# Four of 32 float64 weight tiles loaded and decoded inside the first block of the second MLP

## The chip, the cores and the metric

The kernel runs on one core of one Trainium2 chip. The metric is device time in microseconds (us) of one execution, taken as the median of several runs. Every time below that is not a median of runs comes from one profiled execution of the kernel before.

## The reference

The computation has three parts on 1536 tokens (2 batches of 768) with 512 features. Retention attention gives the tokens. A mixture of 8 experts (first matrix 512x1024, second 1024x512) takes them, each token going to one expert. A second MLP, which all tokens pass, ends it:

```python
def _moe2_ref(x, w_in, w_out):          # x 1536x512, w_in 512x2048, w_out 2048x512
    h = x @ w_in
    g = h - np.tanh(h)
    return (g @ w_out).astype(np.float32)
```

`w_in` and `w_out` come as float64, since they are scaled by a numpy double. The chip's engines work in float32, so the kernel builds a float32 value from the two 32-bit words of each double.

## The kernel before

**Weight tiles.** `w_in` is cut into 16 tiles of 128 columns and `w_out` into 16 tiles of 128 rows. Tile 2f belongs to `w_in`, tile 2f+1 to `w_out`. Each is 128 partitions by 512 values, 512 KB as float64. Decoding one takes a load into one of two `raw` buffers (`decode_load`), two ScalarE operations for the sign (Identity L132, Sign L133) and two VectorE integer operations for the bits (L135, L136) in `decode_math`, and then in `decode_end` a ScalarE Abs (L144) and a GpSimd multiply (L145) that gives the tile `dw`.

**Splits.** Matmuls of the second MLP run in three passes on a high and a low part of each operand. ScalarE casts a decoded tile to its high part `mh` and VectorE subtracts that to give `ml`: in the expert stage in `m_split` (by L153), in the MLP in `high` and `low` (L1025, L1032).

**Stages.** Attention and routing run first, then a loop of 64 expert steps n (8 experts by 8 slices of the hidden width), then the second MLP. The order of instructions on each engine is the order in which they are written (manual schedule). Decoding is spread over attention (5 tiles) and the expert loop: every fourth step below 16, then every second one. The last four tiles, 28 to 31, are fetched in steps 52 to 58 and decoded in steps 55 to 61. Steps 48 to 63 also split tiles 0 to 15.

**The second MLP.** It has three blocks of 512 tokens (w = 0, 1, 2), each with 16 units f of the hidden width, 48 units n in all. For unit n, F(n) (`m_first`, 12 matmuls of 512 columns at L923) makes the hidden values `mhp` from tile 2f. A chain of five ScalarE operations (`g_head`, `g_body`: Square L932, Square L934, Square L942, Tanh L944, Relu L948) and five VectorE operations (L954, L958, L960, L961, L964) makes g. ScalarE casts g to `gh` (L976) and VectorE makes `gl` (L983), both issued inside the chain of unit n+1. S(n) (`m_second`, 12 matmuls at L1003) uses `gh`, `gl` and tile 2f+1. TensorE's order is F0, F1, F2, F3, S0, S1, F4, S2, F5, S3, F6, S4 and so on.

The place of `gl` in the VectorE order depends on the unit. For chains 1 to 4 (the argument `early`) it stands after the first of the five operations; from chain 5 on it stands after the fourth. A list `fill` holds small VectorE jobs. The first two in it are done after the first and the second operation of the next chain, the rest at its end:

```python
        dve.scalar_tensor_tensor(out=s1, in0=s1, scalar=B1, in1=u, ...)   # L954
        gap()                                  # one job of fill
        if last and early:
            g_low(*last)                       # gl of the unit before
        dve.scalar_tensor_tensor(out=s2, in0=s2, scalar=B2, in1=s1, ...)  # L958
        gap()                                  # one job of fill
```

In the kernel before, the jobs are the `low` splits of tiles 16 to 31. Two tiles per unit are split after chains 5 to 12 (`high` on ScalarE right after the chain, `low` in the next chain), by the rule that 2n+8 tiles are split by unit n. All tiles share a pool of 74 slots of 2 KB per partition.

Of the kernel before, what the change touches and what calls it, by code (L numbers as in the profile page):

```python
# [7 lines left out]
F32 = mybir.dt.float32  # L8
F32R = mybir.dt.float32r
I32 = mybir.dt.int32  # L10
U32 = mybir.dt.uint32
BF16 = mybir.dt.bfloat16
ACTF = mybir.ActivationFunctionType
ALU = mybir.AluOpType
# [9 lines left out]
SGN = 768.0  # L24
# [3 lines left out]
def retention_moe_mlp(ctx: ExitStack, tc: tile.TileContext, q, k, v, lam, w_gate, w1, w2, w_in, w_out, out):  # L28
    nc = tc.nc
    pe, act, dve, pool, sp = nc.tensor, nc.scalar, nc.vector, nc.gpsimd, nc.sync  # L30
    B, H, S, D = q.shape
    NT, DM = out.shape
    E, _, F = w1.shape
# [4 lines left out]
    KD = DM // 128  # L38
    NTT = NT // 128
    EF = F // 128  # L40
    NF = FF // 128
    CAP = 256

    WIDE = (240, 240, 220, 212, 206, 200, 196, 192)
    WT = WIDE[0]
# [9 lines left out]
    def slot(shape, dtype, name):  # L55
        return slp.tile(shape, dtype, tag="sl", name=name)

    def bank(shape, name):
        return ps.tile(shape, F32, tag="ps", name=name)
# [38 lines left out]
    idx = const.tile([128, NTT], I32, name="idx")  # L98
    ysort = const.tile([128, KD, NT + CAP], F32, name="ysort")

# [14 lines left out]
    dec = {}  # L115

    def decode_load(i):
        r = raws[i % 2]
        if i % 2 == 0:
            f = i // 2  # L120
            src = w_in.bitcast(I32)[:, f * 256:(f + 1) * 256].rearrange("(k p) (f t) -> p k f t", p=128, t=2)
            sp.dma_start(out=r, in_=src)
        else:
            f = i // 2
            src = w_out.bitcast(I32)[f * 128:(f + 1) * 128, :].rearrange("p (k f t) -> p k f t", k=KD, t=2)
            sp.dma_start(out=r, in_=src)
# [21 lines left out]
    def split(src, name, new=slot, shape=(128, 512)):  # L148
        shape = list(shape)
        hi = new(shape, F32R, name + "h")  # L150
        lo = new(shape, F32R, name + "l")
        act.copy(out=hi, in_=src)  # L152
        dve.tensor_tensor(out=lo, in0=src, in1=hi.bitcast(F32), op=ALU.subtract)  # L153
        return hi, lo
# [312 lines left out]
    def setup_late():  # L467
# [12 lines left out]
        for e in range(E):  # L480
            pool.memset(wide_f[:, e:e + 1], float(WIDE[e]))
        pool.iota(slots_i, pattern=[[1, CAP]], base=1, channel_multiplier=0)
        dve.tensor_copy(out=slots, in_=slots_i)
# [8 lines left out]
    ebase_i = const.tile([128, E], I32, name="ebase_i")  # L492
    slots_both = slot([128, 2, CAP], F32, "slots")
    slots, slots_i = slots_both[:, 0, :], slots_both[:, 1, :].bitcast(I32)
# [24 lines left out]
    def check_counts():  # L519
        cm = sm([128, E], F32, "cm")  # L520
        dve.tensor_tensor(out=cm, in0=byrank[:, 0, :], in1=wide_f, op=ALU.is_gt)
        cx = sm([128, 1], F32, "cx")
        dve.tensor_reduce(out=cx, in_=cm, axis=AX.X, op=ALU.max)
        few = sm([128, 1], F32, "few")
        dve.tensor_reduce(out=few, in_=ct, axis=AX.X, op=ALU.min)
        dve.scalar_tensor_tensor(out=over, in0=few, scalar=128.0, in1=cx, op0=ALU.is_lt, op1=ALU.max)
# [87 lines left out]
    def first_key(t):  # L614
        key = sm([128, 1], F32, "key")
        dve.scalar_tensor_tensor(out=key, in0=lgs[t][:, 1, 0:1], scalar=1.0, in1=ohs[:, t, 0:1], op0=ALU.add, op1=ALU.mult)
        perm = slot([128, CAP], F32, "perm")
        dve.tensor_scalar(out=perm, in0=slots, scalar1=key, scalar2=None, op0=ALU.is_equal)
# [21 lines left out]
    def e_first(*ns, wd=None):  # L640
# [20 lines left out]
        for n, hs, ls, hp in tiles:  # L661
            if n % 2 == 1:
                for g in range(2):
                    ews.pop((n // 2, g))
            hb = slot([128, 2, CAP], F32R, "hb")
            hh, hl = hb[:, 0, 0:wd], hb[:, 1, 0:wd]
# [6 lines left out]
    def e_second(n, col=None, wd=None):  # L673
# [4 lines left out]
        if f == 0:  # L678
            ys[e] = [bank([128, 2, CAP], "yp") for _ in range(KD)]
        for kk in range(KD):  # L680
# [24 lines left out]
    def y_split(w):  # L705
        r = []
        o, width = wins[w]
        per = 512 // width
        for kk in range(0, KD, per):
            hi, lo = split(ysort[:, kk:kk + per, o:o + width], "y", shape=[128, per, width])  # L710
            r += [(hi[:, i, :], lo[:, i, :]) for i in range(per)]
        yhl[w] = r
# [4 lines left out]
    nd = [0]  # L717

    nl = [0]

    def decode_fetch():
        if nl[0] < min(nd[0] + 2, 2 * NF):
            decode_load(nl[0])
            nl[0] += 1

    def decode_step():
        if nd[0] < 2 * NF:
            decode_math(nd[0])
            nd[0] += 1

# [4 lines left out]
    with tc.manual_schedule():  # L735
# [53 lines left out]
        t = NTT - 1  # L789
# [46 lines left out]
    pre = [0]  # L836
# [14 lines left out]
    with tc.manual_schedule():  # L851
        LAG = 2
        for n in range(NE + LAG):
            if n < NE:
                if n == 40:
                    check_counts()
                if n == 4:
                    token_table()
                if n >= 6 and n % 2 == 0 and n < 6 + 2 * (NTT + 1):
                    token_scatter((n - 6) // 2)  # L860
                if n == 1 or n % EF == 0 and 0 < n // EF < E - 1:
                    x_load(n // EF + 1)
                fetch(n)
                if n == 0:
                    e_split1(1, 0)
                    e_first(0, 1)
                elif n > 1:
                    e_first(n)
                if n % 2 == 0:
                    e_split1(n // 2 + 1, 1)  # L870
                else:
                    e_split1((n + 3) // 2, 0)
                e_split2(n)
                if n % EF == 4 and n // EF + 1 < E:
                    x_trans(n // EF + 1, rows_of(n // EF + 1))
                decode_flush()
                if n % (4 if n < 16 else 2) == 1:
                    decode_step()
                if n % (4 if n < 16 else 2) == 0:
                    decode_fetch()  # L880
                if n >= NE - 16 and pre[0] < nd[0] - 3:
                    m_split(pre[0])
                    pre[0] += 1
            if n == 0:
                finish_routing()
            if n >= LAG and (n < 4 or (n - LAG) % EF > 0):
                if n > 4 and (n - LAG) % EF == 1:
                    e_second(n - LAG - 1)
                e_second(n - LAG)
        while nd[0] < 2 * NF:  # L890
            decode_fetch()
            decode_step()
            decode_flush()
# [120 lines left out]
    def second_mlp(fresh):  # L1014
        seq = []
        for w, (o, width) in enumerate(wins):
            per = 512 // width
            units = [tuple(range(f, f + per)) for f in range(0, NF, per)]
            seq += [(w, fs) for fs in units]
        LAG = 2  # L1020

        def high(i):
            w = dec[i]
            hi = slot([128, 512], F32R, "mh")
            act.copy(out=hi, in_=w.rearrange("p k f -> p (k f)"))  # L1025
            whl[i] = hi

        def low(i):
            w = dec.pop(i)
            hi = whl[i]  # L1030
            lo = slot([128, 512], F32R, "ml")
            dve.tensor_tensor(out=lo, in0=w.rearrange("p k f -> p (k f)"), in1=hi.bitcast(F32), op=ALU.subtract)  # L1032
            whl[i] = (hi, lo)

        y_split(0)
        while fresh and pre[0] < 2:
            m_split(pre[0])
            pre[0] += 1
        steps = []
        for n in range(len(seq)):  # L1040
            steps.append(("F", n))
            if n >= LAG:
                steps.append(("S", n - LAG))
        n = len(seq)
        steps += [("S", i) for i in range(n - LAG, n)]
        i = steps.index(("F", n - 1))
        assert steps[i - 1] == ("S", n - 4)
        steps[i - 1:i + 1] = [("F", n - 1), ("S", n - 4), ("G", n - 1)]
        a, b = steps.index(("S", 0)), steps.index(("F", LAG + 1))
        steps[a], steps[b] = steps[b], steps[a]  # L1050
        fill = []
        for kind, n in steps:
            if kind == "S":
                m_second(*seq[n], fresh)
                continue
            w, fs = seq[n]
            if kind == "F":
                m_first(w, fs)
                if n + 1 < len(seq) and seq[n + 1][0] != w:
                    y_split(w + 1)  # L1060
                if n == len(seq) - 1:
                    continue
            g_head(w, fs)
            g_body(w, fs, fill, seq[n - 1] if n else None, n <= 4)
            if fresh:
                while pre[0] < min(2 * n + 8, 2 * NF):
                    high(pre[0])
                    fill.append(lambda i=pre[0]: low(i))
                    pre[0] += 1
            if n == len(seq) - 1:  # L1070
                g_high(w, fs)
                g_low(w, fs)
# [130 lines left out]
```

## Time and profile before

| | us |
|---|---|
| median of 3 runs | 554.06 |
| lowest and highest run | 551.78, 557.68 |
| profiled execution, its own time | 554.32 |
| its span (first to last instruction) | 552.6 |
| TensorE busy in the span | 527.9 (96%) |
| VectorE busy | 422.2 (76%) |
| ScalarE busy | 356.7 (65%) |
| GpSimd busy | 114.6 (21%) |

The profile is one execution seen by the hardware profiler. TensorE's busy time has modelled ends, so a busy TensorE is not one at its peak; what can be read surely is when it sat idle and who ended that. The expert loop ends and the second MLP starts near 273 us of the span; the first block of the MLP (units 0 to 15) lasts until about 356 us.

### The profile page before, as it was taken

What the parts mean: (1) busy time and instruction counts of PE and PEld (TensorE: products, weight loads), DVE (VectorE), ACT (ScalarE), POOL (GpSimd) and SP (SyncE); (2) the same over time, 40 slices, a digit from 0 to 9 for tenths busy, and PEclk for the clock granted to TensorE, in tenths of its full rate; (3) what the DMA queues carried; (4) which work ended last, traced back from release to release, by engine and by line L of the source; (5) the groups of instructions that cost most, each with busy time, mean ns of one, the idle gap of its engine ahead of it and who ended that gap; (6) DMA issues with size and microseconds to landing.
All of it is one profiled execution on the core that took longest, in us unless ns stands there. A gap on an engine that the chain in (4) does not pass through costs nothing.

```text
span 552.6 us, 9795 instructions
## 1 busy us (share of the span) xinstructions
PE 527.9 (96%) x3373; PEld 457.7 (83%) x3373; DVE 422.2 (76%) x814; ACT 356.7 (65%) x734; POOL 114.6 (21%) x163
## 2 busy tenths in 40 slices
PE   6999998899999899999899999999999999999991
PEld 6888777899999899999788888888888888888881
DVE  5877976889786657799978889887767687767670
ACT  2456755677686667789776787856565667565650
POOL 2256852324253222222200000002000003000002
PEclk7899998999999999999999999999999999999996
DMA  5999868599999999997000000001000001000002
GB/s 146 235 275 259 240 206 282 173 278 216 279 346 268 311 315 315 297 299 252 1 2 1 1 0 1 1 17 61 1 1 2 0 1 76 1 1 0 2 0 81
DMA packets 75411, 72.41 MB, mean 131 GB/s; under 512 B 30127, under 2 KB 60847, under 8 KB 75353
## 3 DMA queue, kind: packets, MB, share of 16 engines
q1 hardware_dynamic: 73001, 65.40, 41.0%
q0 software_dynamic: 2352, 6.31, 3.2%
q8 instruction: 28, 0.46, 0.4%
q14 instruction: 30, 0.25, 0.1%
HBM read 63.29 MB, written 8.39 MB: 130 GB/s over the span
## 4 chain that ended last, share of the span: by engine, by line
PE 66%; issue 16%; DMA 6%; DVE 5%; ACT 3%; POOL 2%; SPq 1%; DVEq 0%; ACTq 0%; POOLq 0%
PE mhp L923 17%; PE outp L1003 16%; PE yp L684 7%; PE ehp L651 7%; PE yp L683 4%; DMA raw<-in_moe_w_out_dram 3%; PE op L348 2%; PE ehp L658 2%; PE sp L300 2%; PE ehp L660 2%; PE ehp L659 2%; DMA k<-in_k_dram 1%; PE op L337 1%; POOL out_dram L68 1%; PE xtp L577 1%
## 5 line engine op out<-in xcount | busy, mean ns | idle before, releaser
L684 PE MATMUL yp<-hb,w2h 128*128 128x480 f32 (+6 forms) x256 | 83.8, 376 | 0.0
L932 ACT ACTIVATE u<-mhp 128x512 f32<-128x512 f32 x48 | 28.7, 597 | 83.0 <-PE mhp L923 82.9
L683 PE MATMUL yp<-hb,w2l 128*128 128x240 f32 (+6 forms) x256 | 73.2, 286 | 4.7 <-DVE w2l L153 2.4
L923 PE MATMUL mhp<-yh,mh 128*128 128x512 f32 x192 | 75.5, 393 | 0.9 <-ACT yh L152 0.8
L1003 PE MATMUL outp<-mh,gh 128*128 128x512 f32 x192 | 75.1, 396 | 0.0
L923 PE MATMUL mhp<-yh,ml 128*128 128x512 f32 x192 | 75.0, 390 | 0.0
L1003 PE MATMUL outp<-mh,gl 128*128 128x512 f32 x192 | 74.9, 395 | 0.0
L1003 PE MATMUL outp<-ml,gh 128*128 128x512 f32 x192 | 74.9, 395 | 0.0
L954 DVE SCALAR_TENSOR_TENSOR s<-s,u 128x512 f32<-128x512 f32 x48 | 33.2, 691 | 47.1 <-ACT s L934 47.1
L145 POOL TENSOR_TENSOR dw<-da,sg 128x512 f32<-128x512 f32 x32 | 43.2, 1349 | 113.7 <-ACT da L144 90.3
L68 POOL DMA_INDIRECT out_dram<-ysort,idx x12 | 11.7, 974 | 262.0 <-ACT ysort L1008 258.3
L651 PE MATMUL ehp<-xh,w1r 128*128 128x212 f32 (+4 forms) x320 | 60.2, 333 | 0.0
L153 DVE TENSOR_TENSOR w2l<-w2r,w2h 128x512 fp32r<-128x512 f32 x64 | 54.5, 852 | 3.2
L651 PEld LDWEIGHTS ehp<-xh,w1r 128*128 128x128 f32 x320 | 55.8, 190 | 0.1
L683 PEld LDWEIGHTS yp<-hb,w2l 128*128 128x128 f32 x256 | 49.7, 194 | 6.0 <-DVE w2l L153 3.2
L923 PE MATMUL mhp<-yl,mh 128*128 128x512 f32 x192 | 51.4, 390 | 0.0
L684 PEld LDWEIGHTS yp<-hb,w2h 128*128 128x128 f32 x256 | 49.2, 192 | 1.9
L923 PEld LDWEIGHTS mhp<-yh,mh 128*128 128x128 f32 x192 | 36.1, 188 | 10.5 <-ACT yh L152 2.5
L1003 PEld LDWEIGHTS outp<-mh,gl 128*128 128x128 f32 x192 | 36.2, 189 | 9.5 <-DVE gl L983 0.3
L1003 PEld LDWEIGHTS outp<-ml,gh 128*128 128x128 f32 x192 | 36.1, 188 | 8.6
L923 PEld LDWEIGHTS mhp<-yh,ml 128*128 128x128 f32 x192 | 36.0, 188 | 7.7
L1003 PEld LDWEIGHTS outp<-mh,gh 128*128 128x128 f32 x192 | 36.0, 188 | 7.7
(158 smaller groups left out, 1160.2 us busy)
## 6 DMA issues: line engine op xcount, KB each, us to landing
w1r<-in_moe_w_dram SPq DMA_DIRECT2D x64, 256.0 KB, 6.1
w2r<-in_moe_w_dram SPq DMA_DIRECT2D x64, 256.0 KB, 6.7
raw<-in_moe_w_in_dram SPq DMA_DIRECT2D x16, 512.0 KB, 4.3
raw<-in_moe_w_out_dram SPq DMA_DIRECT2D x16, 512.0 KB, 7.2
q<-in_q_dram SPq DMA_DIRECT2D x12, 256.0 KB, 7.2
v<-in_v_dram SPq DMA_DIRECT2D x12, 256.0 KB, 5.4
k<-in_k_dram SPq DMA_DIRECT2D x11, 256.0 KB, 5.6
xr<-xs_d SPq DMA_DIRECT2D x8, 256.0 KB, 5.3
```

The costliest lines, as they stand in the source:

```text
L68: ins = pool.indirect_dma_start(out=dst[:, :], out_offset=bass.IndirectOffsetOnAxis(ap=ix.bitcast(U32), axis=0), in_=src, in_offset=None)
L145: pool.tensor_tensor(out=w, in0=a.bitcast(F32), in1=sg, op=ALU.mult)
L153: dve.tensor_tensor(out=lo, in0=src, in1=hi.bitcast(F32), op=ALU.subtract)
L300: pe.matmul(sps[j][:, hp, :], lhsT=kt[js, hp, :], rhs=qt[hp // 2][js, hp % 2, :], start=True, stop=True)
L348: pe.matmul(op[64 * j:64 * j + 64, hp, :], lhsT=vx[:, h, :], rhs=ats[j][:, hp, :], start=(not inter and hp == 0), stop=True, skip_group_ch ...
L651: pe.matmul(hp, lhsT=w[:, i, n % 2, :], rhs=hs[g][:, i, 0:wd], start=(g + i == 0), stop=(g + i == 2))
L683: pe.matmul(o[:, 0, 0:wd], lhsT=bl[:, ks], rhs=hb[:, 0, 0:wd], start=(f == 0), stop=False, skip_group_check=True)
L684: pe.matmul(o[:, :, 0:wd], lhsT=bh[:, ks], rhs=hb[:, :, 0:wd], start=False, stop=(f == EF - 1), skip_group_check=True)
L923: pe.matmul(hp[:, j, :], lhsT=a[:, sl], rhs=b, start=(i == 0), stop=(i == 3 * KD - 1))
L932: act.activation(out=u, in_=hp, func=ACTF.Square)
L954: dve.scalar_tensor_tensor(out=s1, in0=s1, scalar=B1, in1=u, op0=ALU.add, op1=ALU.mult)
L1003: pe.matmul(outp[w][i], lhsT=a[:, sl], rhs=b, start=(fs[j] == 0 and m == 0), stop=done)
```

## The change

`ND = 28`: the expert loop decodes tiles 0 to 27 only. The tiles 28 to 31 are loaded, decoded and split inside the first block of the MLP. Tile 28+j is loaded (two transfers of 256 KB into two slots) after chain 2j, its sign operations go behind chain 2j+1 on ScalarE and its bit operations into `fill` as two jobs of half a tile each, and its Abs and GpSimd multiply go behind chain 2j+2. The rule for the splits is now max(n+16, 2n+5), so that one tile per unit is split after chains 1 to 11 and two after chains 12 and 13.

```diff
+    ND = 28
@@ decode_fetch, decode_step, the loop's tail
-        if nl[0] < min(nd[0] + 2, 2 * NF):
+        if nl[0] < min(nd[0] + 2, ND):
-        if nd[0] < 2 * NF:
+        if nd[0] < ND:
-        while nd[0] < 2 * NF:
+        while nd[0] < ND:
@@ second_mlp
+        def late_load(i):
...
+            late[i] = [slot([128, 2, 128, 2], I32, "late") for _ in range(2)]
+            for g in range(2):
+                sp.dma_start(out=late[i][g], in_=src[:, 2 * g:2 * g + 2])
+
+        def late_math(i, fill):
+            r = late.pop(i)
+            sg = slot([128, KD, 128], F32, "sg")
+            a = slot([128, KD, 128], I32, "da")
+            for g in range(2):
+                gs = slice(2 * g, 2 * g + 2)
+                lo, hi = r[g][:, :, :, 0], r[g][:, :, :, 1]
+                act.activation(out=sg[:, gs], in_=hi.bitcast(F32), func=ACTF.Identity, bias=SGN)
+
+                def bits(gs=gs, lo=lo, hi=hi):
+                    dve.tensor_scalar(out=a[:, gs], in0=hi, scalar1=3, scalar2=0x40000000, op0=ALU.logical_shift_left,
+                                      op1=ALU.bitwise_xor)
+                    dve.scalar_tensor_tensor(out=a[:, gs], in0=lo, scalar=29, in1=a[:, gs], op0=ALU.logical_shift_right,
+                                             op1=ALU.bitwise_or)
+
+                fill.append(bits)
+            act.activation(out=sg, in_=sg, func=ACTF.Sign, bias=-SGN)
+            late[i] = (sg, a)
+
+        def late_end(i):
+            sg, a = late.pop(i)
+            act.activation(out=a.bitcast(F32), in_=a.bitcast(F32), func=ACTF.Abs)
+            pool.tensor_tensor(out=sg, in0=a.bitcast(F32), in1=sg, op=ALU.mult)
+            dec[i] = sg
+
+        def late_work(n, fill):
+            for j, at_ in enumerate((1, 3, 5, 7)):
+                i = ND + j
+                if n == at_ - 1:
+                    late_load(i)
+                if n == at_:
+                    late_math(i, fill)
+                if n == at_ + 1:
+                    late_end(i)
@@ after g_body of unit n
-                while pre[0] < min(2 * n + 8, 2 * NF):
+                late_work(n, fill)
+                while pre[0] < min(max(n + 16, 2 * n + 5), 2 * NF) and pre[0] in dec:
                     high(pre[0])
                     fill.append(lambda i=pre[0]: low(i))
                     pre[0] += 1
```

## Rows read from the trace of the kernel before

**Rows 1.** The head of the profile's page.

```profile
span 552.6 us, 9795 instructions
```

**Rows 2.** Busy time by stretch: length; PE, PEld, DVE, ACT, POOL; clock, DMA share, GB/s.

```profile
190.00:200.00 10.00, 7.99 (x43) 7.89 (x44) 6.80 (x14) 7.71 (x18) 1.89 (x2) 0.83 1.04 345
...
240.00:269.50 29.50, 29.50 (x189) 28.89 (x188) 28.99 (x50) 25.22 (x56) 8.57 (x6) 1.00 0.60 197
269.50:286.30 16.80, 14.84 (x66) 11.34 (x66) 13.15 (x23) 12.20 (x25) 0.44 (x1) 1.00 0.00 1
292.00:540.00 248.00, 248.00 (x1077) 201.76 (x1076) 192.18 (x300) 160.63 (x296) 8.66 (x17) 1.00 0.03 9
```

**Rows 3.** TensorE in order of time, waits where experts end: start, us; idle before.

```profile
270.55 0.36 PE L683 MATMUL yp<-hb,w2l 128*128 128x192 f32 x1 [1.02 <-DVE w2l L153]
...
274.02 0.50 PE L923 MATMUL mhp<-yh,mh 128*128 128x512 f32 x1 [0.58 <-ACT yh L152]
```

**Rows 4.** VectorE in order of time, end of the expert loop.

```profile
266.18 0.68 DVE L153 TENSOR_TENSOR w2l<-w2r,w2h 128x512 fp32r<-128x512 f32 x1
266.78 0.41 DVE L135 TENSOR_SCALAR da<-raw 128x512 int32<-128x512 int32 x1
267.23 0.69 DVE L136 SCALAR_TENSOR_TENSOR da<-raw,da 128x512 int32<-128x512 int32 x1
...
268.71 1.78 DVE L153 TENSOR_TENSOR w2l<-w2r,w2h 128x512 fp32r<-128x512 f32 x1
```

**Rows 5.** GpSimd in order of time, two of its 32 multiplies.

```profile
193.62 1.27 POOL L145 TENSOR_TENSOR dw<-da,sg 128x512 f32<-128x512 f32 x1 [5.08 <-ACT da L144]
...
268.66 1.28 POOL L145 TENSOR_TENSOR dw<-da,sg 128x512 f32<-128x512 f32 x1 [3.22 <-ACT da L144]
```

**Rows 6.** VectorE in order of time, beside the multiply at 193.62.

```profile
193.81 0.37 DVE L668 SCALAR_TENSOR_TENSOR hb<-ehp,hb 128x206 fp32r<-128x206 f32 x1
```

**Rows 7.** ScalarE in order of time, end of the expert loop.

```profile
264.64 0.68 ACT L132 ACTIVATE sg<-raw 128x512 f32<-128x512 f32 x1
265.35 0.63 ACT L133 ACTIVATE sg<-sg 128x512 f32<-128x512 f32 x1
...
266.40 0.32 ACT L667 ACTIVATE hb<-ehp 128x192 fp32r<-128x192 f32 x1
```

**Rows 8.** VectorE in order of time, first operations of chains 2 to 5.

```profile
287.29 0.67 DVE L954 SCALAR_TENSOR_TENSOR s<-s,u 128x512 f32<-128x512 f32 x1
...
291.44 0.68 DVE L954 SCALAR_TENSOR_TENSOR s<-s,u 128x512 f32<-128x512 f32 x1
...
296.03 0.69 DVE L954 SCALAR_TENSOR_TENSOR s<-s,u 128x512 f32<-128x512 f32 x1 [0.24 <-ACT s L934]
...
301.57 0.69 DVE L954 SCALAR_TENSOR_TENSOR s<-s,u 128x512 f32<-128x512 f32 x1 [0.55 <-ACT s L934]
...
304.37 0.68 DVE L983 TENSOR_TENSOR gl<-s,gh 128x512 fp32r<-128x512 f32 x1
```

**Rows 9.** TensorE in order of time, third matmul of S4, first with gl.

```profile
306.08 0.40 PE L1003 MATMUL outp<-mh,gl 128*128 128x512 f32 x1
```

**Rows 10.** VectorE in order of time, the two splits inside chain 13.

```profile
346.56 0.68 DVE L1032 TENSOR_TENSOR ml<-dw,mh 128x512 fp32r<-128x512 f32 x1
...
347.76 0.68 DVE L1032 TENSOR_TENSOR ml<-dw,mh 128x512 fp32r<-128x512 f32 x1
```

**Rows 11.** TensorE in order of time, second matmul of F14, first with ml.

```profile
347.50 0.39 PE L923 MATMUL mhp<-yh,ml 128*128 128x512 f32 x1
```

**Rows 12.** TensorE in order of time, two other waits and the matmul behind each.

```profile
101.54 0.38 PE L683 MATMUL yp<-hb,w2l 128*128 128x240 f32 x1 [1.38 <-DVE w2l L153]
...
192.01 0.54 PE L683 MATMUL yp<-hb,w2l 128*128 128x206 f32 x1 [2.24 <-DVE ysort L694]
```

**Rows 13.** The tile raw: time from a load's issue to its landing.

```profile
DMA to landing us min/median/max: 4.3/6.8/9.2
```

**Rows 14.** ScalarE groups by line: the function table's load.

```profile
L262 ACT ACT_TABLE_LOAD x1 | 1.3, 1283 | 0.8 <-PEq L1187 0.8
```

More of the change, by code (lines that the diff above doesn't have):

```diff
@@ L1033, in low @@
             whl[i] = (hi, lo)
+        late = {}
+        def late_load(i):
+            f = i // 2
+            if i % 2 == 0:
+                src = w_in.bitcast(I32)[:, f * 256:(f + 1) * 256].rearrange("(k p) (f t) -> p k f t", p=128, t=2)
+            else:
+                src = w_out.bitcast(I32)[f * 128:(f + 1) * 128, :].rearrange("p (k f t) -> p k f t", k=KD, t=2)
+            late[i] = [slot([128, 2, 128, 2], I32, "late") for _ in range(2)]
[31 more added lines that the diff above has]
+                    late_end(i)
         y_split(0)
```

## The prediction

> **What bounds the kernel now.** I read the page first, then the busy time by stretch, then each engine in order of time around the places that the change touches. TensorE is busy almost throughout, so a change is worth what TensorE waits less or more. The stretches say where it waits [rows 2]: not at all in the last 29.5 us of full expert work, 2.0 us between 269.5 and 286.3 us, and not at all from 292 us to 540 us. So work that leaves the expert loop can give back at most what lies in the middle row, and work that enters the MLP costs as soon as it makes TensorE wait, for good, since no later slack takes it up.
>
> The other engines are the second thing to see. VectorE is busy 28.99 of 29.50 us at the end of the expert loop; in the MLP it is busy 192.2 of 248 us [rows 2]. The change moves work from the stretch where VectorE is full to one with more room, and the first units of that stretch are the question.
>
> **What leaves the expert loop.** A decode there costs VectorE its two bit operations, 0.41 and 0.69 us, and as much again through GpSimd: a split that should take 0.68 us took 1.78 us when it started inside a multiply of 1.28 us [rows 4, 5]. That is 1.1 + 1.1 = 2.2 us per tile, 8.8 us for four. TensorE sees of it only the one wait at 270.55, 1.02 us, for a `w2l` that stood behind just such a blocked subtraction [rows 3, 4]. With 8.8 us less before it, VectorE is on time there, and all of the 1.02 us goes. The next wait, 0.58 us for `yh`, hangs on the last expert's sums and stays [rows 3]. The 2 MB of loads that go delay nobody, as TensorE had no wait in that stretch [rows 2]. Gain: 1.0 us (0 if something else is late at the same place).
>
> **What enters the MLP, by engine.** ScalarE gets per late tile two Identity of half a tile, a Sign and an Abs. Whole ones take 0.68 and 0.63 us. A half tile lies between the 0.32 us of 192 columns and the 0.68 us of 512, some 0.4 us [rows 7], and a second one overlaps the first by 0.1 us; so 0.4 + 0.3 + 0.6 = 1.3 us behind chains 1, 3, 5, 7 and 0.5 us behind chains 2, 4, 6, 8. No function-table load comes with them: there is one in the whole execution, although Sign, Exp and Tanh all run [rows 14].
>
> VectorE gets two jobs per late tile, each a shift on half a tile and an OR on half a tile. The OR took 0.69 us for 512 columns, a like operation 0.37 us for 206 [rows 4, 6], so 0.42 us for 256. Operations that don't wait for each other start 0.09 us before the last ends (0.69 us long, 0.60 apart [rows 8, 10]), which leaves 0.33 us. The shift, 0.41 us whole, has no second size: between half and all of it, I take 0.32 us. A job is 0.65 us, a tile 1.3 us, within 1.05 us (both halve exactly) and 2.1 us (neither gets shorter).
>
> It also gets the splits earlier: one `low` of 0.60 us in every chain from 2 on, where before there was none below chain 6.
>
> **Chains 2 to 5.** VectorE runs chains 1 to 3 without rest: 4.15 us each, from 287.29 to 291.44 [rows 8]. Into chain 2 come the two jobs of tile 28 and one `low`: 4.15 + 1.3 + 0.6 = 6.05 us. Chain 3 gets a `low`: 4.75 us. Chain 4 gets tile 29 and a `low`: 6.05 us. ScalarE cannot run ahead either, for its Abs stands behind chain 2 and waits for the second job, and the squares of chain 3 queue behind it. From 287.4 the starts become 293.5, 298.2 and, for chain 5, 304.3, where before it was 301.57 [rows 8]: 2.7 us late.
>
> Chain 5 is the first with `gl` in fourth place. Before, `gl` of unit 4 began 2.80 us after the chain's start [rows 8]; with a `low` in the gap (0.6 us, 0.2 us of which was a pause between dependent operations) it begins 3.2 us after, at 307.5, and ends at 308.2. S4's third matmul, which needs it, stood at 306.08 [rows 9].
>
> S1 and S2 meet the same delay before that. Units are 5.54 us apart (296.03 to 301.57 [rows 8]), so their third matmuls stood at 289.46 and 295.0. `gl` of unit 1 comes behind the first job and a `gh` that ScalarE's 1.8 us of new work pushes back, and ends at 289.7; that of unit 2 ends at 295.6. I count 0.3 us for each. S4 then stands at 306.7 and waits 1.5 us. Together 2.1 us.
>
> **Chains 6 and 8.** VectorE now alternates 5.6 us (with a tile) and 4.6 us, under the 5.54 us of a unit on average, so it does not fall further behind. What is left is GpSimd's multiply, which falls on `gl` of units 5 and 7: it starts some 0.8 us after the second job, `gl` is due 1.2 us after, and the multiply lasts 1.28 us [rows 5]. `gl` loses 0.75 us, of which I count 0.5 us as TensorE's each time: 1.0 us.
>
> The other operations beside a multiply are a choice: an `hb` with one operand in PSUM took 0.37 us inside a multiply, a subtraction with both in SBUF 1.78 us for 0.68 us [rows 4 to 6]. The chain's last operation (a copy under a mask) has its mask in SBUF and its data in PSUM, and I let it pass like `hb`; if it were blocked, chains 2 and 4 would be 0.7 us longer and S4 would wait up to 1.4 us more. The Trainium skill, "SBUF — State Buffer", section "Who interferes with whom", says that only two-port modes and operations with two SBUF inputs contend with GpSimd; by it the copy passes and the sum stays, and the two rows agree with it.
>
> **Chains 13 and 14.** The new rule for splits reaches tile 28 after chain 12 and tile 30 after chain 13, each as the second of a pair. The two `low` of a pair stand 1.2 us apart, with one operation between, and the second began at 347.76 and took 0.68 us, so it ended at 348.44 [rows 10]. F14, which uses tile 28, had its first matmul with a low part at 347.50 [rows 11]. In the kernel before, that tile had been split long ago; now F14 waits 0.9 us, and F15 the same for tile 30. Sum 1.9 us, between 0 (should the pair come sooner) and 2.0 us.
>
> **Loads.** Tile 28 must have landed by 284.3 us, when ScalarE ends chain 1. Its slots come from some 20 that the expert loop leaves; if the last of them is free only at 273.4 us, the slowest load seen, 9.2 us [rows 13], lands at 282.6. Hidden, with 1.7 us to spare; the later tiles have more.
>
> **Sum.** −1.0 + 2.1 + 1.0 + 1.9 = +4.0 us on the profiled execution's 554.32 us (span 552.6 us [rows 1] and 1.7 us around it), which stands 0.26 us above the median. On the median: 554.06 + 4.0 = 558.1 us. With jobs of 1.05 us per tile and no wait in F14 and F15, the sum is about +1 us; with 2.1 us per tile S4 alone waits 1.6 us more, and with the copy blocked the sum is +7 us.
>
> **Rivals.** *It is covered, and slightly faster.* The place is S4: `gl` of 0.68 us, 3.2 us behind the start, is in time for 306.08 if chain 5 starts by 302.2, 0.6 us late instead of 2.7 us [rows 8, 9]. Then no S waits, and if F14 and F15 find their low parts too, only the gain is left: 553.1 us (555.0 us if they wait). For it: VectorE's 22% of free time in the MLP [rows 2]. Against it: that free time lies behind chain 4, and chains 1 to 3 have none.
>
> *The clock falls.* A wait of 2.24 us at 192.01 us was followed by a matmul of 0.54 us for 206 columns; after a wait of 1.38 us one of 240 columns took 0.38 us [rows 12]. In the 10 us around the first the granted clock is 0.83 on average [rows 2], as 3.4 us at 1.2 GHz and the rest at 2.4 GHz make it, which costs 1.7 us. My 1.5 us at S4 lies between the two. Should it be longer than I think, the time is 558.1 + 1.7 = 559.8 us, or 561 us with the longer wait itself.
>
> *The loads come late.* If a late tile's slots come free only with the MLP's own work, ScalarE stands at the Identity and with it the chains behind it. A load of 6.8 us [rows 13] issued behind chain 2's end instead of before it would delay chain 4 by 2 to 3 us for each tile: 563 us and more. Against it: 20 free slots.
>
> **Chances.** The forecast with a wait at S4 and one at F14: 0.50 (555 to 560.5 us). Covered: 0.25. Clock: 0.18. Late loads: 0.04. Faster than 553 us for a reason that I don't see: 0.03. The range, 553.0 to 561.5 us, takes in all but the last two and the outer ends of the clock's case. The runs before lie 6 us apart, so about 1% (5.5 us) is what a measurement of this kernel can tell from no change. Slower by that, over 559.6 us: most of the clock's case, the late loads, and a tenth or so of the forecast: 0.23. Faster by it, under 548.5 us: more than all waits of the middle row [rows 2], 0.03. Within: 0.74.
>
> **What the profile after would show.** Right: no wait for `w2l` near 270 us; TensorE idle before S4's third matmul for 1 to 2 us with `gl` as its releaser; idle of 0.9 us before the second matmuls of F14 and F15, released by the split `ml`; chain 5's first VectorE operation some 2.7 us later against F4 than before. Wrong: no idle between 286 and 356 us (covered), a granted clock below 1.00 in the MLP (clock), ScalarE idle before an Identity with a load as releaser (late loads).

## The result: 0.9% slower

The changed kernel's median is 559.74 us against 554.55 us for the kernel before, timed beside each other in 12 runs each. The ratio is 1.0088, with a 95% interval from 1.0061 to 1.0115: slower by 3.4 to 6.4 us. (A ratio here is estimated from the single runs, so it is not exactly the quotient of the two medians.) The profiled execution took 557.63 us, its span 555.9 us. One execution of the experiments below, the profiled one of the second version with one late tile, ran at a mean granted clock of 0.748 (span 651.0 us) and is left out of that kernel's median and ratio.

The busy time by stretch of the changed kernel (length; TensorE, its weight loads, VectorE, ScalarE, GpSimd; clock; share of the DMA engines; GB/s), with the borders put where its stages lie:

```profile
240.00:266.50 26.50, 26.50 (x173) 26.50 (x172) 21.60 (x40) 17.37 (x40) 3.09 (x2) 1.00 0.42 140
266.50:283.40 16.90, 16.01 (x78) 12.78 (x77) 12.04 (x22) 12.59 (x27) 0.00 (x0) 1.00 0.21 63
283.40:360.00 76.60, 72.57 (x306) 56.60 (x305) 67.61 (x114) 59.50 (x113) 5.21 (x5) 1.00 0.03 8
360.00:540.00 180.00, 180.00 (x782) 146.41 (x781) 135.21 (x209) 111.33 (x205) 8.57 (x16) 1.00 0.03 12
```

Against [rows 2], VectorE at the end of the expert loop is no longer full (21.60 of 26.50 us), and TensorE's waits between the loop and the MLP fell from 2.0 to 0.9 us. In the first block of the MLP, where it had no wait, it now has 4.0 us of them.

TensorE in order of time, changed kernel, the matmuls that waited since the end of the expert loop (in brackets idle time and who ended it; those below 0.15 us are left out):

```profile
271.23 0.50 PE L924 MATMUL mhp<-yh,mh 128*128 128x512 f32 x1 [0.58 <-ACT yh L153]
272.88 0.50 PE L924 MATMUL mhp<-yh,mh 128*128 128x512 f32 x1 [0.17 <-ACT yh L153]
305.51 0.50 PE L1004 MATMUL outp<-mh,gl 128*128 128x512 f32 x1 [1.40 <-DVE gl L984]
311.66 0.50 PE L1004 MATMUL outp<-mh,gl 128*128 128x512 f32 x1 [0.35 <-DVE gl L984]
323.61 0.50 PE L1004 MATMUL outp<-mh,gl 128*128 128x512 f32 x1 [0.59 <-DVE gl L984]
349.49 0.50 PE L924 MATMUL mhp<-yh,ml 128*128 128x512 f32 x1 [0.84 <-DVE ml L1033]
356.19 0.50 PE L924 MATMUL mhp<-yh,ml 128*128 128x512 f32 x1 [0.84 <-DVE ml L1033]
```

The wait for `w2l` of [rows 3] is gone. The three waits for `gl` are those of S4, S5 and S7, the two for `ml` those of F14 and F15.

Idle time understates what such a wait costs. A better count comes from the start times of the first matmul of each F and S in the two traces: how much later than before does the next one start? The same count serves all experiments below; it is read to some 0.03 us.

| place | later than before, us | forecast, us |
|---|---|---|
| last expert steps to F0 (5.95 before, 4.35 after) | −1.60 | −1.0 |
| S1, S2 | +0.35, +0.30 | +0.3, +0.3 |
| S4 | +1.66 | +1.5 |
| S5, S7 | +0.61, +0.86 | +0.5, +0.5 |
| F14, F15 | +1.16, +1.14 | +0.95, +0.95 |
| rest of the MLP (48 units) | +0.1 | 0 |
| sum | +4.6 | +4.0 |

The sum of 4.6 us is 0.83% of 554.55 us, and the runs give 0.88%. The two profiled spans lie only 3.3 us apart because of something else: TensorE's waits for VectorE's `ysort` near 168 and 192 us differ from execution to execution (2.24 us in the kernel before, 0.73 and 1.72 us here), and with them the clock. In the kernel before the matmul behind such a wait ran at 1.2 GHz [rows 12]; in this execution the granted clock stayed at 1.00, that is 2.4 GHz, from 190 to 200 us, and the last expert steps were reached 1.19 us sooner. The second experiment, whose expert stage is that of the kernel before, had neither wait and reached them 3.84 us sooner: a difference of this size comes without the change.

### The profile page after: what moved, and what is told of

Same layout as the page of the kernel before. It is cut to its first block, busy times and chain, and to the rows that moved or that the text cites. A ratio compares the mean times of both kernels' runs of the same rounds, so it can differ in the third digit from the quotient of the medians.

```text
span 555.9 us, 9816 instructions
## 1 busy us (share of the span) xinstructions
PE 528.6 (95%) x3373; PEld 455.4 (82%) x3373; DVE 421.9 (76%) x822; ACT 357.7 (64%) x738; POOL 113.2 (20%) x163
## 4 chain that ended last, share of the span: by engine, by line
PE 55%; issue 16%; DMA 9%; ACT 8%; DVE 7%; POOL 2%; SPq 1%; ACTq 0%; POOLq 0%; DVEq 0%
PE mhp L924 13%; PE outp L1004 12%; PE ehp L652 7%; PE yp L685 7%; DMA raw<-in_moe_w_out_dram 5%; PE yp L684 3%; PE op L349 2%; PE sp L301 2%; PE op L338 1%; DMA k<-in_k_dram 1%; POOL out_dram L69 1%; PE ehp L661 1%; PE ehp L660 1%; PE ehp L659 1%; DMA w1r<-in_moe_w_dram 1%
## 5 line engine op out<-in xcount | busy, mean ns | idle before, releaser
L685 PE MATMUL yp<-hb,w2h 128*128 128x480 f32 (+6 forms) x256 | 82.3, 371 | 0.0
L146 POOL TENSOR_TENSOR dw<-da,sg 128x512 f32<-128x512 f32 x28 | 37.3, 1332 | 96.4 <-ACT da L145 91.5
L154 DVE TENSOR_TENSOR w2l<-w2r,w2h 128x512 fp32r<-128x512 f32 x64 | 52.9, 827 | 3.8 <-ACT w2h L153 0.2
```

Of the source, the lines that this page charges most:

```text
L146: pool.tensor_tensor(out=w, in0=a.bitcast(F32), in1=sg, op=ALU.mult)
L685: pe.matmul(o[:, :, 0:wd], lhsT=bh[:, ks], rhs=hb[:, :, 0:wd], start=False, stop=(f == EF - 1), skip_group_check=True)
```

## The experiments

Each has one part of the change, or the change with one cause altered. Differences are start-to-start times of the same matmuls, as in the table, and ratios to the kernel before stand beside them where the kernel was timed. The third, fourth and fifth kernel were run once each, for the trace (553.91, 556.91 and 551.82 us), and have no ratio.

**The expert stage's part alone.** The two added lines stand in `second_mlp` ahead of the units.

```diff
-                late_work(n, fill)
-                while pre[0] < min(max(n + 16, 2 * n + 5), 2 * NF) and pre[0] in dec:
+                while pre[0] < min(2 * n + 8, 2 * NF):
+        for j in range(ND, 2 * NF):
+            dec[j] = dec[j - 4]
```

> Only the expert stage's part of the change: 28 tiles are decoded, tiles 28 to 31 are neither loaded nor decoded, and the MLP uses tiles 24 to 27 in their place with the splits of the kernel before (so part of w_in and w_out is left out of the result). Theory: VectorE is on time at the end of the expert loop, no wait for w2l near 270 us, and no wait in the MLP. The two traces put the last expert steps to F0 at 5.95 us before and 4.35 us after, so 1.6 us less than the kernel before, ratio 0.997. Rival, that the first matmul of the MLP came 2.8 us sooner after the change because of the change: 2.8 us less. Rival, that the decode hides under TensorE anyway: no difference, and the wait for w2l still there.

Measured: 548.9 against 551.1 us, ratio 0.9957 (0.9942 to 0.9973). The last expert steps to F0 took 1.60 us less than before, and no F or S of the MLP moved against F0 by more than 0.05 us. No wait for `w2l` is left; the only waits over 0.15 us between the last experts and the second block are those for `yh` that the kernel before has too [rows 3]:

```profile
268.73 0.50 PE L924 MATMUL mhp<-yh,mh 128*128 128x512 f32 x1 [0.58 <-ACT yh L153]
270.37 0.50 PE L924 MATMUL mhp<-yh,mh 128*128 128x512 f32 x1 [0.17 <-ACT yh L153]
```

So the gain is 1.6 us by the trace. The rival of 2.8 us falls by the trace, though its ratio, 0.995, lies inside the interval as well.

**The new rule for the splits alone.**

```diff
-                while pre[0] < min(2 * n + 8, 2 * NF):
+                while pre[0] < min(max(n + 16, 2 * n + 5), 2 * NF):
```

> Only the new rule for the splits, max(n+16, 2n+5), all 32 tiles decoded in the expert loop. Theory: F14 and F15 wait for the second split of a pair, 0.84 us of idle each and 1.15 us from start to start each, so 2.3 us more than the kernel before; one low in chains 2 to 4 makes chain 5 some 0.3 us late, and S4 does not wait. Rival, that the earlier splits by themselves overload VectorE: S4 waits over 0.5 us as well and the sum is 3 us or more. Rival, that the pairs only wait because the chains before them are late: no wait at F14 and F15, no difference.

Measured: 552.66 against 551.1 us, ratio 1.0032 (1.0012 to 1.0053). F14 and F15 cost 1.15 and 1.10 us more, the whole MLP 2.4 us; S4 does not wait, nor does any S before it. In the trace of this kernel, TensorE's waits:

```profile
266.70 0.36 PE L683 MATMUL yp<-hb,w2l 128*128 128x192 f32 x1 [1.02 <-DVE w2l L153]
...
344.64 0.50 PE L923 MATMUL mhp<-yh,ml 128*128 128x512 f32 x1 [0.84 <-DVE ml L1032]
351.33 0.50 PE L923 MATMUL mhp<-yh,ml 128*128 128x512 f32 x1 [0.84 <-DVE ml L1032]
```

The wait for `w2l` is that of the kernel before, and the two for `ml` are those of the changed kernel to the hundredth. They come from the rule alone. VectorE's chain 5 starts 27.57 us behind F0 (270.18 us), where the kernel before has 27.55 us [rows 3, 8], so the 0.3 us of delay that I expected did not come:

```profile
297.75 0.69 DVE L954 SCALAR_TENSOR_TENSOR s<-s,u 128x512 f32<-128x512 f32 x1 [0.49 <-ACT s L934]
```

**No multiply on GpSimd.** The four tiles' signs are left out.

```diff
-            pool.tensor_tensor(out=sg, in0=a.bitcast(F32), in1=sg, op=ALU.mult)
-            dec[i] = sg
+            dec[i] = a.bitcast(F32)
```

> The changed kernel without GpSimd's multiply of the four late tiles (their signs are left out of the result). Theory, that the multiply holds VectorE's subtraction for gl: gl of units 5 and 7 takes 0.69 us instead of 1.47 us, the waits at S5 and S7 (0.61 and 0.86 us from start to start after the change) go, and the waits at S4, F14 and F15 stay (1.66, 1.15, 1.15 us). Rival, that S5 and S7 wait because VectorE has too much to do there: they stay over 0.4 us each.

Measured, by the trace: S5 and S7 do not wait; S4 costs 1.62 us, F14 and F15 1.1 us each. VectorE in order of time, `gl` of units 5 and 7 in the changed kernel; then GpSimd's multiply beside the first of them; then VectorE's same two operations without the multiply:

```profile
310.14 1.47 DVE L984 TENSOR_TENSOR gl<-s,gh 128x512 fp32r<-128x512 f32 x1
...
322.09 1.47 DVE L984 TENSOR_TENSOR gl<-s,gh 128x512 fp32r<-128x512 f32 x1
```

```profile
309.76 1.29 POOL L1070 TENSOR_TENSOR sg<-da,sg 128x512 f32<-128x512 f32 x1 [8.71 <-ACT da L1069]
```

```profile
307.80 0.68 DVE L984 TENSOR_TENSOR gl<-s,gh 128x512 fp32r<-128x512 f32 x1
...
319.12 0.68 DVE L984 TENSOR_TENSOR gl<-s,gh 128x512 fp32r<-128x512 f32 x1
```

The subtraction that begins inside a multiply of 1.29 us ends 0.8 us late. Without the multiply it doesn't, and the two waits go with it.

**Abs and multiply one unit later.**

```diff
-                if n == at_ + 1:
+                if n == at_ + 2:
```

> The changed kernel with Abs and multiply of each late tile one unit later, so that ScalarE never waits for VectorE's bit jobs at the Abs. Theory, VectorE's own load in chains 2 to 4 makes chain 5 late: S4 still waits over 1 us (1.40 us of idle after the change). Rival, the Abs that blocks ScalarE's queue (1.5 us twice) delays the squares and through them the chains: S4's wait falls below 0.4 us. F14 and F15 wait 0.84 us of idle in both.

Measured, by the trace: S4 waits longer, not less, and S5 and S7 no longer wait; the MLP loses 5.5 us where the changed kernel loses 6.2. TensorE's wait at S4, and the start of chain 5 on VectorE:

```profile
305.97 0.50 PE L1004 MATMUL outp<-mh,gl 128*128 128x512 f32 x1 [1.85 <-DVE gl L984]
```

```profile
302.04 0.68 DVE L955 SCALAR_TENSOR_TENSOR s<-s,u 128x512 f32<-128x512 f32 x1
```

F0 started at 271.19 us here and at 271.23 us in the changed kernel, where chain 5 started at 301.56 us. ScalarE's queue was free of its two waits at the Abs, and chain 5 came 0.5 us later. But this kernel has the multiply later too. It now falls on the second operation of chain 3, which has both inputs in SBUF (GpSimd, then VectorE):

```profile
292.00 1.67 POOL L1070 TENSOR_TENSOR sg<-da,sg 128x512 f32<-128x512 f32 x1 [44.16 <-ACT da L1069]
```

```profile
292.44 1.78 DVE L959 SCALAR_TENSOR_TENSOR s<-s,s 128x512 f32<-128x512 f32 x1
```

The same operation took 0.69 us in the changed kernel, so this costs 1.1 us. Without it chain 5 would have started, by an estimate from these rows, some 29.8 us behind F0: 0.6 us sooner than in the changed kernel (30.33 us), and still 2.2 us later than in the kernel before (27.55 us). So the blocked queue, which the prediction names as a second reason, makes some 0.6 of the 2.8 us by which chain 5 is late, and VectorE's own work the larger part. S4, 1.40 us idle in the changed kernel, would by this estimate still have waited some 0.8 us, over the rival's 0.4 and under the theory's 1 us; no run shows it apart from the multiply.

**The old rule for the splits, with all four tiles late.**

```diff
-                while pre[0] < min(max(n + 16, 2 * n + 5), 2 * NF) and pre[0] in dec:
+                while pre[0] < min(2 * n + 8, 2 * NF) and pre[0] in dec:
```

> The changed kernel with the rule for the splits of the kernel before, 2n+8 (late tiles only once they are decoded). Theory, that S4 waits because jobs and splits together overload VectorE in chains 2 to 4: without the three splits chain 5 starts about 1.8 us sooner and S4 does not wait; F14 and F15 do not wait, since no pair comes late. In return chains 6 and 8 hold a tile and two splits, 6.2 us and the multiply, so that S5, S6, S7 and S8 wait some 0.6 to 0.9 us each; the MLP loses 2.5 to 4 us instead of 6.2. Rival, that the bit jobs alone make S4 wait: its wait stays above 1 us.

Measured, by the trace: S1 to S4 and F14, F15 don't wait; S5 costs 1.56, S6 0.46, S7 0.40 and S8 0.48 us, the MLP 3.0 us in all. VectorE's chain 5 with the `gl` of unit 4, then the start of chain 6 and the `gl` of unit 5, with F0 at 268.63 us:

```profile
297.03 0.68 DVE L955 SCALAR_TENSOR_TENSOR s<-s,u 128x512 f32<-128x512 f32 x1
299.81 0.68 DVE L984 TENSOR_TENSOR gl<-s,gh 128x512 fp32r<-128x512 f32 x1
...
302.46 0.69 DVE L955 SCALAR_TENSOR_TENSOR s<-s,u 128x512 f32<-128x512 f32 x1 [1.30 <-ACT s L935]
...
306.20 1.46 DVE L984 TENSOR_TENSOR gl<-s,gh 128x512 fp32r<-128x512 f32 x1
```

Chain 5 starts 28.40 us behind F0, where the changed kernel has 30.33 and the kernel before 27.55 us. So the late tiles without the three splits make chain 5 0.9 us late, and the three splits without the late tiles (second experiment) leave it in its place. The two together make 2.8 us: the pauses that take up the splits alone are gone once the bit jobs stand there. Neither alone makes S4 wait; both together do. S5 cost more than the 0.6 to 0.9 us that were expected: two splits on ScalarE beside the sign operations also push the squares of chain 6 back. VectorE waits 1.30 us for them, and chain 6 starts 0.7 us later than in the kernel before.

**The pairs one unit sooner.**

```diff
-                while pre[0] < min(max(n + 16, 2 * n + 5), 2 * NF) and pre[0] in dec:
+                while pre[0] < min(max(n + 16, 2 * n + 7), 2 * NF) and pre[0] in dec:
```

> The changed kernel with the rule max(n+16, 2n+7): tiles 28 and 30 are split one unit sooner, everything else stays. Theory: the waits at F14 and F15 go (1.15 us each from start to start), those at S1, S2, S4, S5, S7 stay; 2.3 us less than the changed kernel, 2 to 3 us more than the kernel before, ratio 1.004 to 1.005. Rival, that VectorE would then be late at S10 to S12: waits appear there and most of the 2.3 us stays.

Measured: 554.3 against 552.44 us, ratio 1.0029 (1.0006 to 1.0053). F14 and F15 don't wait. S1, S2, S4, S5 and S7 cost 0.37, 0.31, 1.64, 0.62 and 0.86 us as in the changed kernel. S14 costs 0.4 us that it did not cost there, so 1.9 of the 2.3 us come back and the MLP loses 4.3 us. The rule leaves the split of tile 31 for chain 14, which is 0.4 us longer by it than in the kernel before:

```profile
351.60 0.69 DVE L1033 TENSOR_TENSOR ml<-sg,mh 128x512 fp32r<-128x512 f32 x1
```

With the gain of 1.6 us that is +2.65 us or 0.48%; the runs give 0.29%, with 0.48% inside their interval. The ratio lies under the 1.004 to 1.005 that were expected.

**`gl` in second place up to chain 9.** On top of the run before:

```diff
-            g_body(w, fs, fill, seq[n - 1] if n else None, n <= 4)
+            g_body(w, fs, fill, seq[n - 1] if n else None, n <= 9)
```

> As the run with the rule max(n+16, 2n+7), and with gl in second place in chains 5 to 9 too, where the changed kernel has it in fourth. Theory, that S4, S5 and S7 wait only because gl stands behind jobs, four chain operations and the multiply: gl of unit 4 ends some 2 us sooner, and these three waits fall below 0.3 us; S1 and S2 keep 0.35 and 0.30 us. The MLP loses about 0.7 us, the end of the expert stage gains 1.6, sum 0.9 us less than the kernel before, ratio 0.998. Rival, that VectorE has too much work in chains 2 to 8 whatever the order: waits move to S5 to S8 or to the F behind them, and the MLP still loses 2 us or more.

Measured: 551.7 against 552.44 us, ratio 0.9988 (0.9961 to 1.0014). The waits at S4, S5 and S7 are gone entirely. VectorE, chain 5 (F0 at 266.85 us):

```profile
297.18 0.70 DVE L955 SCALAR_TENSOR_TENSOR s<-s,u 128x512 f32<-128x512 f32 x1
298.52 0.69 DVE L984 TENSOR_TENSOR gl<-s,gh 128x512 fp32r<-128x512 f32 x1
```

The chain starts 30.33 us behind F0, as late as in the changed kernel, but `gl` begins 1.34 us after it and not 3.21 us. So VectorE can do the whole work; what cost S4, S5 and S7 time was where `gl` stood in it. S1, S2, S9 and S14 still cost 0.36, 0.30, 0.35 and 0.42 us, 1.5 us in all where I expected 0.7, and that takes back nearly the whole gain of 1.6 us. (S9's `gl` is the first to stand in fourth place again; S14 has the split of the run before.)

**One late tile, two versions.** Tile 31 is loaded after chain 2 and gets its Abs and multiply after chain 6.

```diff
-    ND = 28
+    ND = 31
-            for j, at_ in enumerate((1, 3, 5, 7)):
+            for j, at_ in enumerate((4,)):
-                if n == at_ - 1:
+                if n == at_ - 2:
-                if n == at_ + 1:
+                if n == at_ + 2:
-                while pre[0] < min(max(n + 16, 2 * n + 5), 2 * NF) and pre[0] in dec:
+                while pre[0] < min(2 * n + 6, 2 * NF) and pre[0] in dec:
```

> Only the last tile, 31, is moved into the MLP: its load after chain 2, its sign after chain 4, its bits in chain 5, its Abs and multiply after chain 6, and the splits by the rule 2n+6, so that chain 6 has none. Theory: the end of the expert stage needs only that VectorE is spared the last tile's 2.2 us, so the wait for w2l goes as with four tiles, 1.6 us less; the MLP has no wait, since chains 5 and 6 have a pause of 1 us before gl is needed. Ratio 0.997. Rival, that all four tiles are needed for the gain: a wait for w2l of over 0.3 us stays.

Measured, first version: 551.24 against 552.44 us, ratio 0.9979 (0.9951 to 1.0007). The last expert steps to F0 took 1.59 us less: one tile gives the whole gain. In the MLP there is one wait that I had not foreseen:

```profile
358.57 0.50 PE L1004 MATMUL outp<-mh,gl 128*128 128x512 f32 x1 [0.57 <-DVE gl L984]
```

It is S14's, 0.85 us from start to start. The rule 2n+6 puts a pair of splits into chain 14, right ahead of the four splits of `y` for the second block. The second version moves that pair to chains 2 and 3:

```diff
-                while pre[0] < min(2 * n + 6, 2 * NF) and pre[0] in dec:
+                while pre[0] < min(max(min(n + 16, 18), 2 * n + 8), 2 * NF) and pre[0] in dec:
```

> As the run with one late tile, with two of the splits moved from chain 14 to chains 2 and 3: the rule is max(min(n+16, 18), 2n+8). Theory, that S14 waited there (0.57 us of idle, 0.85 us from start to start) because chain 14 held a pair of splits just ahead of the four splits of y for the next block: that wait goes, chains 2 and 3 take their one split each without a wait as in the run with the new rule alone, and the MLP loses under 0.3 us. Sum 1.6 us less than the kernel before, ratio 0.997. Rival, that S14 waits because of the late tile itself: 0.5 us or more of idle stay at S14.

Measured, second version: 550.15 against 552.01 us, ratio 0.9983 (0.9963 to 1.0003). The same kernel was profiled and timed once more.

> The same kernel as the run before with one late tile and the rule max(min(n+16, 18), 2n+8), for a profile of it at full clock: theory, no idle of TensorE in the MLP before S14's third matmul over 0.1 us, the last expert steps to F0 in 4.35 us, ratio 0.997; rival, 0.5 us or more of idle at S14.

Measured: 550.19 against 553.34 us, ratio 0.9936 (0.9911 to 0.9961). The stretch of this kernel from the last experts to the end of the first block:

```profile
267.00:360.00 93.00, 92.11 (x406) 74.24 (x405) 81.41 (x133) 69.85 (x132) 1.33 (x2) 1.00 0.02 7
```

TensorE's 0.9 us of waits are all those for `yh` before and in F0; S14 has none. The last expert steps to F0 took 1.60 us less than before and the MLP 0.14 us more, together −1.5 us or −0.26%. That lies inside the first interval and just above the second (the two intervals of one kernel, 0.9963 to 1.0003 and 0.9911 to 0.9961, do not overlap, so an interval here tells less than its width says). By the trace it is the best of the kernels that compute everything.

**Only the last multiply moved.** The kernel before, with Abs and multiply of tile 31 behind chain 4 of the MLP (the last two lines, after `g_body`):

```diff
-    def decode_flush():
+    def decode_flush(held=(2 * NF - 1,)):
         for i in sorted(dpart):
-            decode_end(i)
+            if i not in held:
+                decode_end(i)
...
+                if n == 4:
+                    decode_flush(())
```

> The kernel before with one thing moved: Abs and GpSimd's multiply of tile 31 stand behind chain 4 of the MLP instead of the end of the expert loop; its load, sign and bits stay there. Theory, that the wait for w2l at the end of the expert loop is made by that multiply, which holds VectorE's subtraction for 1.1 us: the subtraction takes 0.69 us, the wait shrinks from 1.02 us to under 0.3 us, and the gain is 1.2 to 1.6 us of the 1.6 us that four tiles give; in chain 4 the multiply meets operations with data in PSUM and costs nothing. Ratio 0.997 to 0.998. Rival, that VectorE is late there by the sum of its work: the wait stays over 0.6 us and the gain is under 0.6 us.

Measured: 551.11 against 552.01 us, ratio 0.9989 (0.9969 to 1.0009). The last expert steps to F0 took 1.11 us less and the wait for `w2l` is gone. VectorE, the subtraction that took 1.78 us in [rows 4]:

```profile
266.76 0.68 DVE L153 TENSOR_TENSOR w2l<-w2r,w2h 128x512 fp32r<-128x512 f32 x1
```

So 1.1 of the 1.6 us that the change gains hang on one GpSimd instruction, a little less than the 1.2 to 1.6 us that were expected. The multiply itself costs nothing in chain 4, as expected. S14 costs 0.4 us, which was not expected, so the trace comes to −0.7 us in all, and the interval takes in no difference. In chain 14 the second operation waits 0.47 us for ScalarE's Tanh, which it doesn't read,

```profile
348.15 0.69 DVE L959 SCALAR_TENSOR_TENSOR s<-s,s 128x512 f32<-128x512 f32 x1 [0.47 <-ACT t L945]
```

and chain 15's `gl` follows that late. What ties it to the Tanh was not tried.

## Why the prediction was right, point by point

**Where the time goes.** All places named in the MLP were right: S1, S2, S4, S5, S7, F14 and F15 wait, and no other place by more than 0.1 us. The wait for `w2l` goes too. The parts add up: 1.6 us less from the expert stage (first experiment), 2.3 us more from the rule's pairs (second), 1.5 us from the multiply (third), the rest from VectorE's load with `gl` late in it (fourth, fifth and seventh).

**The new operations.** A bit job was to take 0.65 us. VectorE in order of time, changed kernel, chain 2 from its first operation to the start of chain 3:

```profile
284.67 0.69 DVE L955 SCALAR_TENSOR_TENSOR s<-s,u 128x512 f32<-128x512 f32 x1
285.28 0.29 DVE L1058 TENSOR_SCALAR da<-late 128x256 int32<-128x256 int32 x1
285.60 0.42 DVE L1060 SCALAR_TENSOR_TENSOR da<-late,da 128x256 int32<-128x256 int32 x1
286.18 0.69 DVE L984 TENSOR_TENSOR gl<-s,gh 128x512 fp32r<-128x512 f32 x1 [0.15 <-ACT gh L977]
...
289.45 0.76 DVE L965 COPY_PREDICATED s<-m,mhp 128x512 f32<-128x512 int32 x1
290.09 0.69 DVE L1033 TENSOR_TENSOR ml<-dw,mh 128x512 fp32r<-128x512 f32 x1
290.69 0.69 DVE L955 SCALAR_TENSOR_TENSOR s<-s,u 128x512 f32<-128x512 f32 x1
```

The shift takes 0.29 us and the OR 0.42 us, near the 0.32 and 0.42 us estimated from operations of other lengths, and chain 2 lasts 6.02 us (forecast 6.05). Chain 5 then starts 2.78 us late against F0 (forecast 2.7). Against F4, which the prediction names for this sign, it is 2.4 us, since F4 stands behind S1 and is itself 0.36 us late.

**The copy under a mask.** The line at 289.45 also settles the choice beside GpSimd. A multiply ran there:

```profile
288.88 1.30 POOL L1070 TENSOR_TENSOR sg<-da,sg 128x512 f32<-128x512 f32 x1 [41.00 <-ACT da L1069]
```

The copy took 0.76 us inside it, and 0.73 to 0.76 us without it, so it passes. The rule cited from the Trainium skill's "SBUF — State Buffer", section "Who interferes with whom", holds here on both sides: the copy, with one input in SBUF, passes, and operations with both inputs there took 1.47 us (`gl`, third experiment) and 1.78 us (fourth) inside a multiply, for 0.68 and 0.69 us without.

**What was mis-sized.** The term is the price of a wait. For the gain I took the idle time shown, and for the new waits a late operand's end minus the time at which the matmul stood before. From start to start each wait costs some 0.26 us more than its idle time: S4 1.66 for 1.40 us, S5 0.61 for 0.35, S7 0.86 for 0.59. The rows show where it lies. Matmuls start 0.23 us apart but last 0.39 us by the modelled end, and idle is counted from that end, so 0.16 us are hidden in it; and the matmul after a wait takes 0.50 us, with the next one 0.33 us behind it instead of 0.23 us:

```profile
305.51 0.50 PE L1004 MATMUL outp<-mh,gl 128*128 128x512 f32 x1 [1.40 <-DVE gl L984]
305.84 0.39 PE L1004 MATMUL outp<-mh,gh 128*128 128x512 f32 x1
306.07 0.39 PE L1004 MATMUL outp<-ml,gh 128*128 128x512 f32 x1
```

The matmul that waited 1.02 us for `w2l` in the kernel before [rows 3] costs 1.28 us by the same count. The other 0.31 us of the gain come from a second wait there, which the prediction does not have. It stands in the kernel before at

```profile
272.01 0.36 PE L683 MATMUL yp<-hb,w2l 128*128 128x192 f32 x1
```

with less than 0.05 us of idle shown: this matmul starts 0.41 us behind the one before it, in the changed kernel 0.20 us, and the next one loses 0.10 us more. The tenth experiment leaves this one in place, which is most of why it gains 1.1 us and not 1.6.

The seven waits of the MLP were forecast at 5.0 us and cost 6.1; what went was forecast at 1.0 us and gave 1.6. The two errors, 1.1 and 0.6 us, have opposite signs in the sum, so that it is only 0.6 us off: that is luck.

**The rivals.** *Covered* did not come, but the seventh experiment shows how near it was: with `gl` in second place S4, S5 and S7 cost nothing, at the same load. The prediction's condition for it, VectorE less than 0.6 us late at chain 5, holds only for `gl` in fourth place. *The clock*: the measured median, 559.74 us, lies nearer to this rival's 559.8 us than to the forecast of 558.1 us, but the profiled execution shows nothing of it: 1.40 us of idle at S4 left the granted clock at 1.00 in the whole MLP. Of the 1.6 us above the forecast, 0.5 us are the kernel before, which had 554.55 us in the runs beside it and not 554.06, and 0.6 us the sizes above; the rest is within the interval. A longer wait of this execution, 1.72 us, stands before no fall either:

```profile
192.48 0.36 PE L684 MATMUL yp<-hb,w2l 128*128 128x206 f32 x1 [1.72 <-DVE ysort L695]
```

The same matmul took 0.54 us in [rows 12]. *Late loads*: the loads were issued from 263.2 to 288.2 us, the first ones ahead of the MLP, and no Identity waited for one.

**A second reason.** The prediction has ScalarE's queue, blocked at the Abs, as a second cause in chains 2 to 4, with no term of its own in the sum. The fourth experiment puts it at some 0.6 of the 2.8 us, by an estimate, since it moved the multiply as well.

## What to carry to other kernels

Find out which instruction ends the wait that one wants to remove before moving a whole piece of work: here one tile of the four gave the whole gain at that place, and moving one GpSimd multiply 1.1 of its 1.6 us. When work goes to an engine with idle time, ask first where in that engine's order the result stands that the busiest engine waits for: 22% of free time in the MLP [rows 2] did not help while `gl` stood behind four operations and the new jobs, and with `gl` moved ahead the same work cost nothing there. A rule that spreads work evenly (one split per unit) has to be read at its last units, against the latest moment at which each piece is wanted: two pieces that came one unit late cost 2.3 of the 2.4 us that the rule alone cost.

## What the runs showed of the hardware that I had not expected

TensorE's idle time in the profile is about 0.26 us short of what a wait costs from start to start (five waits between 0.35 and 1.40 us, each 0.26 to 0.32 us more), and a wait of 0.3 us can show next to no idle time.

The length of a single wait alone doesn't tell whether TensorE's clock falls behind it. In the profiled execution of the changed kernel the wait of 1.40 us at S4 left the granted clock at 1.00, and so did the one of 1.72 us at 192.48 us. Another of 1.40 us, at 85.81 us, stands before a fall to 0.50, that is 1.2 GHz (the matmul behind it, and the stretch from 86.5 to 89.5 us):

```profile
85.81 1.66 PE L611 MATMUL xtp<-ident,xr 128*128 128x128 f32 x8 [1.40 <-DMA xr<-xs_d]
...
86.50:89.50 3.00, 3.00 (x12) 2.45 (x13) 1.39 (x6) 1.19 (x2) 1.39 (x4) 0.50 0.87 256
```

What makes the difference was not tried.
